# Whole tile loads, overlapping places for K, and products with a zero tile, in a one-token transformer block

## The chip, the cores and the metric

The kernel runs on one core of one Trainium2 chip. The metric is the device time in microseconds of one execution. Before the change it was 202.29 us, the median of three executions (202.23 to 202.43). "Span" below is the length of a profiled execution without its launch, 1.2 to 1.4 us shorter than the time in all executions but five (1.5 to 2.4 us there). The "granted clock" is the share of its full speed at which TensorE was let run; 0.50 is called half clock below.

## The reference

One new token goes through attention over a cache of 4096 keys and values in 32 heads, then through a gated feed-forward block. Cut to what matters:

```python
def reference(A_x, A_k_cache, A_v_cache, A_wq, A_wo, B_x, B_w_gate, B_w_up, B_w_down):
    # x: [1,1,640]; k_cache, v_cache: [1,32,4096,128]; wq: [640,4096]; wo: [4096,640]
    q = (layernorm(x) @ wq)                   # 32 heads of 128
    p = softmax(q . k_cache * 128**-0.5)      # 4096 scores a head
    h = x + (p . v_cache) @ wo
    g, u = layernorm(h) @ w_gate, layernorm(h) @ w_up     # 1728 wide
    return h + (gelu(g) * u) @ w_down
```

All of it is bf16. Nearly every byte is used once: 84.2 MB come from HBM, and 67 MB of them are K and V.

## The kernel before

Eight heads make a tile, and there are four tiles (NG). In a tile, partition 16h+p holds 256 keys of head h, so a tile of K or V is 64 KB in each partition, 8.39 MB in all. VectorE multiplies a quarter of K at a time with the query (`mult`, into `prod`). TensorE adds up the products in groups with an identity as weights (`fold`), VectorE finishes the sums (`total`), ScalarE takes the exponential, VectorE spreads it into `p_bd` (`block`), and TensorE multiplies that with V (`pv`). K has one buffer, filled in halves, and V has one buffer; all large loads are issued from SP (SyncE), in order.

```python
def load_k(j, s):          # K of tile j, half s
    landed["K", j, s] = P.dma("sync", k_all[:, HALF*s : HALF*s+HALF], src[:, HALF*s : HALF*s+HALF],
                              mults.get((j - 1, s, 1)))          # waits for that half's last multiplication
...
lp = P.loop("tensor", range(NG), [
    ("f00", lambda e, j: fold(e, 0), lambda j: [mults[j, 0, 0], reds[j - 1, 1] if j else qa], True),
    ("f01", lambda e, j: fold(e, 1), lambda j: [mults[j, 0, 1]], True),
    ("f10", lambda e, j: fold(e, 0), lambda j: [mults[j, 1, 0], reds[j, 0]], True),
    ("f11", lambda e, j: fold(e, 1), lambda j: [mults[j, 1, 1]], True),
    ("p0", lambda e, j: pv(e, 0), lambda j: [blocks[j, 0], landed["V", j, 0]], True),
    ("p1", lambda e, j: pv(e, 1), lambda j: [blocks[j, 1], seen[j]], True),
    ("h", lambda e, j: head_sum(e, j * 8), lambda j: [evs[j]], True)])
...
for j in range(NG):
    mult(j, 0, 0); mult(j, 0, 1)
    if j < NG - 1: load_k(j + 1, 0)
    mult(j, 1, 0); total(j, 0); mult(j, 1, 1)
    if j < NG - 1: load_k(j + 1, 1)
    block(j, 0); total(j, 1); block(j, 1)
    ...                                       # V of tile j+1, after pvs[j, 1]; the last V in halves
```

After the last tile come W_o (into K's buffer), the gate and up weights (into V's buffer, so after the last `pv`) and w_down, and their products with one column each.

The softmax here doesn't subtract the row's maximum and nothing guards it: scores larger than these inputs give would overflow.

Of the kernel before, what the change touches and what calls it, by code (L numbers as in the profile page):

```python
# [5 lines left out]
FP32 = mybir.dt.float32  # L6
BF16 = mybir.dt.bfloat16
ALU = mybir.AluOpType
ACTF = mybir.ActivationFunctionType
AX = mybir.AxisListType  # L10
# [3 lines left out]
DH = 128  # L14
# [6 lines left out]
NG = 4  # L21
# [143 lines left out]
def held(e, out, lhsT, rhs, start, stop):  # L165

    built = e.matmul(out, lhsT, rhs, start=start, stop=stop)  # L167
    old = built.ins
    bb = e.bass.cur_bb.bb
    new = mybir.InstMatmult(  # L170
        start_tensor_calc=old.start_tensor_calc, stop_tensor_calc=old.stop_tensor_calc, tile_size=old.tile_size,
        tile_position=old.tile_position, ldweights=False, name=old.name, engine=old.engine, debug=old.debug,
        ins=old.ins, outs=old.outs, sync_info=old.sync_info)
    insts = bb.instructions
    assert insts[-1].name == old.name
    del insts[-1]
    insts.append(new)
    return bass.BassInstruction(new)


def bass_sequential_preLN__gqa_block_cached__glu_gated_geglu__decode_kernel(nc, A_x, A_k_cache, A_v_cache, A_wq, A_wo, B_x, B_w_gate, B_w_up, B_w_down, out):
    sb = lambda name, shape, dt: nc.alloc_sbuf_tensor(name, shape, dt)
    k_all = sb("k_all", [128, 2 * 128 * DH], BF16)
    v_all = sb("v_all", [128, 256 * DH], BF16)
    prod = sb("prod", [128, 2, 64, DH], BF16)
    qb = sb("qb", [128, NG, DH], BF16)
    sc = sb("sc", [128, 128], FP32)
    pt = sb("pt", [128, 128], BF16)
    spare = sb("spare", [1, 1], FP32)
    own = sb("own", [128, 4], BF16)  # L190
    own8 = sb("own8", [128, 8], BF16)
    p_bd = sb("p_bd", [128, 2, 128, 8], BF16)
# [43 lines left out]
    ps_z = bank[7]  # L236
# [16 lines left out]
    landed = {}  # L253
    HALF = 128 * DH

    def load_k(j, s):
        src = A_k_cache[0, 8 * j:8 * j + 8, :, :].rearrange("h (p r) d -> (h p) (r d)", p=16)
        landed["K", j, s] = P.dma("sync", k_all[:, HALF * s:HALF * s + HALF], src[:, HALF * s:HALF * s + HALF],
                                  mults.get((j - 1, s, 1)))

    def load_v(j, lo, hi, *after, chan=None):
        src = A_v_cache[0, 8 * j:8 * j + 8, :, :].rearrange("h (p r) d -> (h p) (r d)", p=16)
        ev = P.dma("sync", v_all[:, HALF * lo:HALF * hi], src[:, HALF * lo:HALF * hi], *after, chan=chan)
        for i in range(lo, hi):
            landed["V", j, i] = ev

    load_k(0, 0)
    load_k(0, 1)


    c_xz = GP(lambda e: e.memset(xlnB[:, :, :], 0.0))
# [39 lines left out]
    def idle(eng, n):  # L311

        def fn(e):
            for _ in range(n):
                i = e.nop(hint="n", nofuse=True)
            return i
        return P.op(eng, fn)

    idle("tensor", 56)

    def x_cols(e):
        for c in range(5):
# [36 lines left out]
    AS = lambda fn, *d: P.op("scalar", fn, *d, chan="s")  # L359
    GS = lambda fn, *d: P.op("gpsimd", fn, *d, chan="s")  # L360
    qa = VR(lambda e: e.tensor_copy(qb[:, :, :].rearrange("p g d -> p (g d)"), ps_q), qd)  # L361
    load_v(0, 0, 2, qd, chan="V")


    reds, exps, blocks, evs, folds, seen = {}, {}, {}, {}, {}, {}

    def half(e, i, s, first=True):
        for n in range(8):
            mm = held if n or not first else lambda e, *a, **k: e.matmul(*a, **k)  # L369
            r = mm(e, bank[2 * i + s], id_b[:, :], prod[:, i, 32 * s:32 * s + 32, 16 * n:16 * n + 16], start=(n == 0), stop=(n == 7))  # L370
        return r

    def fold(e, i):
        half(e, i, 0)
        return half(e, i, 1, False)

    def pv(e, s):
        vt = tile3(v_all[:, HALF * s:HALF * s + HALF])
        for b in range(32):
            a = 32 * (b % 4)  # L380
            i = e.matmul(ps_o[a:a + 32, :], p_bd[:, s, 4 * b:4 * b + 4, :].rearrange("p g j -> p (g j)"),  # L381
                         vt[:, 4 * b:4 * b + 4, :], start=(s == 0 and b < 4), stop=(s == 1 and b >= 28))
        return i

    def head_sum(e, at):
# [2 lines left out]
                         start=(r == 0), stop=(r == 3))  # L388
        return i

    def mult(j, s, i):
        kt = tile3(k_all[:, HALF * s:HALF * s + HALF])
        mults[j, s, i] = VM(lambda e: e.tensor_tensor(  # L393
            out=prod[:, i, :, :], in0=kt[:, 64 * i:64 * i + 64, :],
            in1=qb[:, j, :].unsqueeze(1).to_broadcast([128, 64, DH]), op=ALU.mult),
            landed["K", j, s], qa, folds.get((j, 0, i) if s else (j - 1, 1, i)))

    def total(j, s):
        reds[j, s] = VR(lambda e: e.reduce_sum(sc[:, :], ps_f.rearrange("p (g d) -> p g d", d=16), axis=AX.X), folds[j, s, 1],  # L399
                        exps.get((j, 0) if s else (j - 1, 1)))  # L400
        exps[j, s] = AS(lambda e: e.activation(pt[:, :], sc[:, :], ACTF.Exp, bias=zero_t[:, 0:1],  # L401
                                               scale=INV_SQRT_DH, accum_out=RS[:, 2 * j + s:2 * j + s + 1]), reds[j, s], c_eps,
                        blocks.get((j, 0) if s else (j - 1, 1)))

    def block(j, s):
        blocks[j, s] = VB(lambda e: e.tensor_tensor(  # L406
            out=p_bd[:, s, :, :], in0=pt[:, :].unsqueeze(2).to_broadcast([128, 128, 8]),
            in1=own8[:, :].unsqueeze(1).to_broadcast([128, 128, 8]), op=ALU.mult), exps[j, s], c_own8, pvs.get((j - 1, s)))

    T(None, c_idb, c_hs)  # L410
    lp = P.loop("tensor", range(NG), [
        ("f00", lambda e, j: fold(e, 0), lambda j: [mults[j, 0, 0], reds[j - 1, 1] if j else qa], True),
        ("f01", lambda e, j: fold(e, 1), lambda j: [mults[j, 0, 1]], True),
        ("f10", lambda e, j: fold(e, 0), lambda j: [mults[j, 1, 0], reds[j, 0]], True),
        ("f11", lambda e, j: fold(e, 1), lambda j: [mults[j, 1, 1]], True),
        ("p0", lambda e, j: pv(e, 0), lambda j: [blocks[j, 0], landed["V", j, 0]], True),
        ("p1", lambda e, j: pv(e, 1), lambda j: [blocks[j, 1], seen[j]], True),
        ("h", lambda e, j: head_sum(e, j * 8), lambda j: [evs[j]], True)])
    for j in range(NG):
        for s in range(2):  # L420
# [3 lines left out]
    for j in range(NG):  # L424
        mult(j, 0, 0)
        mult(j, 0, 1)
        if j < NG - 1:
            load_k(j + 1, 0)
        mult(j, 1, 0)
        total(j, 0)  # L430
        mult(j, 1, 1)
        if j < NG - 1:
            load_k(j + 1, 1)
        block(j, 0)
        total(j, 1)
        block(j, 1)
        seen[j] = GS(lambda e: e.memset(spare[:, :], 0.0), landed["V", j, 1])  # L437
        if j < NG - 2:
            load_v(j + 1, 0, 2, pvs[j, 1], chan="V")
        elif j == NG - 2:  # L440
            load_v(j + 1, 0, 1, pvs[j, 1], chan="V")
            load_v(j + 1, 1, 2)
        evs[j] = AS(lambda e: e.copy(po_sb[:, :], ps_o), pvs[j, 1])  # L443

    rt = GP(lambda e: e.tensor_tensor(out=RT[:, :, :], in0=RS[:, :].unsqueeze(2).to_broadcast([128, 2 * NG, 8]),
# [1 line left out]
    def z_sum(e):  # L447
        for s in range(2):
# [9 lines left out]
    ap = V(lambda e: e.tensor_copy(aP[:, :], ps_z[:, 32:64]), sp)  # L458


    d_wo = [P.dma("sync", wo_sb[:, i:i + 16, :], A_wo[:, :].rearrange("(p i) n -> p i n", i=32)[:, i:i + 16, :], mults[NG - 1, 1, 1])
            for i in (0, 16)]
    wg_sb = v_all[:, 0:5 * DF].rearrange("p (c n) -> p c n", c=5)
    wu_sb = v_all[:, 5 * DF:10 * DF].rearrange("p (c n) -> p c n", c=5)
# [64 lines left out]
    g6 = V(lambda e: e.tensor_mul(gu[:, :], g_t[:, :], t1[:, :]), g8)  # L529
    g9 = V(lambda e: e.tensor_mul(hm[:, :], gu[:, :], ps_u[:, 0:15]), g6, up)  # L530

    idle("vector", 3)

    def down(ms, qs=range(4)):
        def fn(e):
            for m in ms:
# [52 lines left out]
```

## Time and profile before

| | before |
|---|---|
| time | 202.26 us |
| span of the profiled execution | 200.9 us |
| packets of the load queue, share of 16 engines' span | 97.8% |
| busy: TensorE, VectorE | 57%, 52% |
| mean granted TensorE clock | 0.795 |
| last V half seen, w_up seen, last of w_down seen | 171.34, 193.82, 198.50 us |

The prediction below shows the slices, the chain and the rows that matter. Two more lines of the view of the DMA queue's own waits show why VectorE and TensorE appear in a chain that is otherwise DMA; the columns are who waited, for what, us in total, times and the longest wait.

```profile
SPq L59 <- DVE prod L393: 99.6, 7, 24.3
SPq L59 <- PE psum L381: 43.9, 4, 15.0
```

SP waits for a buffer most of the time, 143.5 us in these two lines. In the kernel before, earlier loads were still in the queue while it waited: the packets of the queue fill 97.8% of the span.

### The profile page before, as it was taken

What the parts mean: (1) busy time and instruction counts of PE and PEld (TensorE: products, weight loads), DVE (VectorE), ACT (ScalarE), POOL (GpSimd) and SP (SyncE); (2) the same over time, 40 slices, a digit from 0 to 9 for tenths busy, and PEclk for the clock granted to TensorE, in tenths of its full rate; (3) what the DMA queues carried; (4) which work ended last, traced back from release to release, by engine and by line L of the source; (5) the groups of instructions that cost most, each with busy time, mean ns of one, the idle gap of its engine ahead of it and who ended that gap; (6) DMA issues with size and microseconds to landing.
All of it is one profiled execution on the core that took longest, in us unless ns stands there. A gap on an engine that the chain in (4) does not pass through costs nothing.

```text
span 200.9 us, 2025 instructions
## 1 busy us (share of the span) xinstructions
PE 115.3 (57%) x982; PEld 30.4 (15%) x738; DVE 103.6 (52%) x56; ACT 9.4 (5%) x27; POOL 6.7 (3%) x36
## 2 busy tenths in 40 slices
PE   0108019667094296696605938566088496674675
PEld 0103000000032000001300000023000001474574
DVE  0200197994601969945149799420798965120320
ACT  2100000000001000000100000001000000100100
POOL 6500000000000000000000000000000000000000
PEclk9999856999858559579965899969669879955555
DMA  8999999999899999999999999899999999999992
GB/s 326 449 406 437 431 450 424 417 431 499 385 444 417 424 522 417 417 417 411 417 424 424 489 457 444 378 411 424 424 450 437 431 444 391 432 436 414 423 402 107
DMA packets 3275, 84.31 MB, mean 420 GB/s; under 512 B 387, under 2 KB 582, under 8 KB 966
## 3 DMA queue, kind: packets, MB, share of 16 engines
q1 hardware_dynamic: 3266, 84.23, 97.8%
q8 instruction: 4, 0.07, 0.1%
q14 instruction: 1, 0.01, 0.0%
q10 hardware_dynamic: 4, 0.00, 0.0%
HBM read 84.23 MB, written 0.00 MB: 419 GB/s over the span
## 4 chain that ended last, share of the span: by engine, by line
DMA 66%; DVE 22%; PE 11%; issue 0%; ACT 0%; SPq 0%; DVEq 0%
DMA k_all<-in_A_k_cache_dram 56%; DVE prod L393 18%; DMA v_all<-in_B_w_up_dram 10%; PE psum L167 7%; DVE sc L399 3%; PE psum L516 1%; PE psum L539 1%; PE psum L381 1%; DVE p_bd L406 1%; PE psum L369 1%; SPq L59 0%; ACT pt L401 0%; ACT out_row L555 0%; DVE hm L530 0%; DVEq L114 0%
## 5 line engine op out<-in xcount | busy, mean ns | idle before, releaser
L393 DVE TENSOR_TENSOR prod<-k_all,qb 128x8192 bf16<-128x8192 bf16 x16 | 70.4, 4421 | 38.0 <-DMA k_all<-in_A_k_cache_dram 33.1
L167 PE MATMUL psum<-prod,id_b 128*128 128x512 bf16 x240 | 66.0, 437 | 0.0
L369 PE MATMUL psum<-prod,id_b 128*128 128x512 bf16 x16 | 7.3, 454 | 45.3 <-DVE prod L393 31.5
L381 PE MATMUL psum<-v_all,p_bd 128*32 128x512 bf16 x256 | 19.4, 464 | 14.2 <-DMA v_all<-in_A_v_cache_dram 11.0
L399 DVE TENSOR_REDUCE sc<-psum 128x128 f32<-128x2048 f32 x8 | 18.3, 2288 | 13.3 <-PE psum L167 13.3
L369 PEld LDWEIGHTS psum<-prod,id_b 128*128 128x128 bf16 x16 | 1.6, 99 | 99.8 <-DVE prod L393 59.4
L381 PEld LDWEIGHTS psum<-v_all,p_bd 128*32 128x32 bf16 x256 | 7.5, 114 | 38.5 <-DMA v_all<-in_A_v_cache_dram 21.8
L406 DVE TENSOR_TENSOR p_bd<-pt,own 128x1024 bf16<-128x1024 bf16 x8 | 9.8, 1222 | 2.2 <-ACT pt L401 2.2
L401 ACT ACTIVATE pt<-sc,zero_t 128x128 bf16<-128x128 f32 x8 | 3.2, 402 | 135.9 <-DVE sc L399 135.9
L352 PE MATMUL psum<-v_all,xlnB 128*32 128x512 bf16 x40 | 4.5, 631 | 6.7 <-DMA v_all<-in_A_wq_dram 6.7
L486 PE MATMUL psum<-aP,k_all 128*128 128x1 bf16 x160 | 6.7, 178 | 2.7 <-DMA k_all<-in_A_wo_dram 2.7
L486 PEld LDWEIGHTS psum<-aP,k_all 128*128 128x128 bf16 x160 | 6.6, 131 | 2.8 <-DMA k_all<-in_A_wo_dram 2.8
L516 PE MATMUL psum<-hlnT,v_all 128*128 128x1 bf16 x150 | 5.5, 173 | 1.2 <-DMA v_all<-in_B_w_up_dram 1.2
L387 PE MATMUL psum<-hs,po_sb 128*128 128x8 f32 x32 | 4.2, 258 | 3.2 <-ACT po_sb L443 3.2
L437 POOL MEMSET spare<- 1x1 f32 x4 | 0.4, 88 | 162.8 <-DMA v_all<-in_A_v_cache_dram 162.8
L361 DVE CAST qb<-psum 128x512 bf16<-128x512 f32 x1 | 0.7, 692 | 9.7 <-PE psum L352 9.7
L516 PEld LDWEIGHTS psum<-hlnT,v_all 128*128 128x128 bf16 x150 | 5.3, 120 | 1.8 <-DMA v_all<-in_B_w_up_dram 1.3
L492 DVE COPY hT<-psum 128x5 f32<-128x5 f32 x1 | 0.2, 166 | 9.6 <-PE psum L486 9.6
L387 PEld LDWEIGHTS psum<-hs,po_sb 128*128 128x128 f32 x32 | 3.9, 191 | 5.1 <-issue 5.1
L323 PE MATMUL psum<-one_bf,x_row 1*128 1x1 bf16 x5 | 0.4, 177 | 7.1 <-DMA x_row<-in_A_x_dram 7.1
L326 DVE COPY xx<-psum 128x5 f32<-128x5 f32 x1 | 0.2, 165 | 7.5 <-PE psum L323 7.5
L443 ACT COPY po_sb<-psum 128x512 f32<-128x512 f32 x4 | 2.3, 585 | 22.3 <-PE psum L381 22.3
(71 smaller groups left out, 28.6 us busy)
## 6 DMA issues: line engine op xcount, KB each, us to landing
k_all<-in_A_k_cache_dram SPq DMA_DIRECT2D x8, 4096.0 KB, 29.1
v_all<-in_A_v_cache_dram SPq DMA_DIRECT2D x2, 4096.0 KB, 28.5
v_all<-in_A_wq_dram SPq DMA_DIRECT2D x1, 5120.0 KB, 15.2
k_all<-in_A_wo_dram SPq DMA_DIRECT2D x2, 2560.0 KB, 17.4
v_all<-in_B_w_gate_dram SPq DMA_DIRECT2D x1, 2160.0 KB, 15.0
v_all<-in_B_w_up_dram SPq DMA_DIRECT2D x1, 2160.0 KB, 19.8
k_all<-in_B_w_down_dram SPq DMA_DIRECT2D x1, 800.0 KB, 22.3
k_all<-in_B_w_down_dram SPq DMA_DIRECT2D x1, 640.0 KB, 20.9
```

Of the source, the lines that this page charges most:

```text
L167: built = e.matmul(out, lhsT, rhs, start=start, stop=stop)
L352: i = e.matmul(ps_q[32 * t:32 * t + 32, :], xlnB[:, c, 32 * a:32 * a + 32], wq_j[:, c, t, a, :, :], start=(c == 0 and a == 0), stop=(c == ...
L369: mm = held if n or not first else lambda e, *a, **k: e.matmul(*a, **k)
L381: i = e.matmul(ps_o[a:a + 32, :], p_bd[:, s, 4 * b:4 * b + 4, :].rearrange("p g j -> p (g j)"), vt[:, 4 * b:4 * b + 4, :], start=(s == 0 a ...
L387: i = e.matmul(ps_a[:, bass.ds(at, 8)], po_sb[:, 128 * r:128 * r + 128], hs[:, r, :], start=(r == 0), stop=(r == 3))
L393: mults[j, s, i] = VM(lambda e: e.tensor_tensor(out=prod[:, i, :, :], in0=kt[:, 64 * i:64 * i + 64, :], in1=qb[:, j, :].unsqueeze(1).to_br ...
L399: reds[j, s] = VR(lambda e: e.reduce_sum(sc[:, :], ps_f.rearrange("p (g d) -> p g d", d=16), axis=AX.X), folds[j, s, 1], exps.get((j, 0) i ...
L401: exps[j, s] = AS(lambda e: e.activation(pt[:, :], sc[:, :], ACTF.Exp, bias=zero_t[:, 0:1], scale=INV_SQRT_DH, accum_out=RS[:, 2 * j + s:2 ...
L406: blocks[j, s] = VB(lambda e: e.tensor_tensor(out=p_bd[:, s, :, :], in0=pt[:, :].unsqueeze(2).to_broadcast([128, 128, 8]), in1=own8[:, :]. ...
L443: evs[j] = AS(lambda e: e.copy(po_sb[:, :], ps_o), pvs[j, 1])
L486: r = e.matmul(ps_p[:, c:c + 1], wo_sb[:, i, c::5], aP[:, i:i + 1], start=False, stop=(i == 31), skip_group_check=True)
L516: i = e.matmul(ps[:, m:m + 1], ws, hlnT[:, c:c + 1], start=(c == 0 and m == 0), stop=(c == 4), skip_group_check=True)
```

## The change

The intent: fewer and larger loads, a K buffer of 80 KB in which the next K may be fetched when three quarters of the present one are used, and products with a tile of zeros in TensorE's waits, which were to keep its clock up. The core of the diff:

```diff
-    k_all = sb("k_all", [128, 2 * 128 * DH], BF16)
+    k_all = sb("k_all", [128, 320 * DH], BF16)
+    K_AT = [0, 64 * DH, 0, 64 * DH]
-    def load_k(j, s):
+    def load_k(j):
+        parts = ((0, 1), (1, 2)) if j == NG - 1 else ((0, 2),)
+        for lo, hi in parts:
+            ev = P.dma("sync", k_all[:, K_AT[j] + HALF * lo:K_AT[j] + HALF * hi], src[:, HALF * lo:HALF * hi],
+                       mults.get((j - 1, 1, 0)), chan=None if lo else "K")
 ...
-    idle("tensor", 56)
+    idle("tensor", 22)
 ...
+    def warm(e, n, load=False):
+        for k in range(n):
+            mm = e.matmul if load and k == 0 else lambda *a, **kw: held(e, *a, **kw)
+            r = mm(ps_z, none_b[:, :], none_b[:, :].unsqueeze(1).to_broadcast([128, 4, 128]), start=True, stop=True)
 ...
     lp = P.loop("tensor", range(NG), [
+        ("wa", lambda e, j: warm(e, 8, True), lambda j: [landed["K", j, 0]], False),
         ("f00", ...), ("f01", ...),
+        ("wb", lambda e, j: warm(e, 12), lambda j: [], False),
         ("f10", ...), ("f11", ...),
-        ("p0", lambda e, j: pv(e, 0), lambda j: [blocks[j, 0], landed["V", j, 0]], True),
-        ("p1", lambda e, j: pv(e, 1), lambda j: [blocks[j, 1], seen[j]], True),
+        ("wc", lambda e, j: warm(e, 14), lambda j: [], False),
+        ("p0", lambda e, j: pv(e, 0), lambda j: [blocks[j, 1], landed["V", j]], True),
+        ("p1", lambda e, j: pv(e, 1), lambda j: [], True),
 ...
         mult(j, 0, 0)
         mult(j, 0, 1)
+        mult(j, 1, 0)
         if j < NG - 1:
-            load_k(j + 1, 0)
-        mult(j, 1, 0)
+            load_k(j + 1)
         total(j, 0)
         mult(j, 1, 1)
 ...
-    d_wo = [... mults[NG - 1, 1, 1]) for i in (0, 16)]
+    d_wo = [... mults[NG - 1, 0, 1]) for i in (0, 16)]
 ...
-    idle("vector", 3)
```

(The small GpSimd instruction `seen`, which stood for the landing of V's second half, is gone with that half; the quarters of even tiles are taken in another order, so that the one outside the next tile's place comes last; the second total of an even tile is two instructions. All V loads are whole.)

More of the change, by code (lines that the diff above doesn't have):

```diff
@@ L188, in bass_sequential_preLN__gqa_block_cached__glu_gated_geglu__decode_kernel @@
     pt = sb("pt", [128, 128], BF16)
-    spare = sb("spare", [1, 1], FP32)
     own = sb("own", [128, 4], BF16)
@@ L254, in bass_sequential_preLN__gqa_block_cached__glu_gated_geglu__decode_kernel, with load_v @@
     HALF = 128 * DH
-    def load_k(j, s):
+    K_AT = [0, 64 * DH, 0, 64 * DH]
+    def load_k(j):
         src = A_k_cache[0, 8 * j:8 * j + 8, :, :].rearrange("h (p r) d -> (h p) (r d)", p=16)
-        landed["K", j, s] = P.dma("sync", k_all[:, HALF * s:HALF * s + HALF], src[:, HALF * s:HALF * s + HALF],
-                                  mults.get((j - 1, s, 1)))
-    def load_v(j, lo, hi, *after, chan=None):
-        src = A_v_cache[0, 8 * j:8 * j + 8, :, :].rearrange("h (p r) d -> (h p) (r d)", p=16)
-        ev = P.dma("sync", v_all[:, HALF * lo:HALF * hi], src[:, HALF * lo:HALF * hi], *after, chan=chan)
-        for i in range(lo, hi):
-            landed["V", j, i] = ev
-    load_k(0, 0)
-    load_k(0, 1)
+        parts = ((0, 1), (1, 2)) if j == NG - 1 else ((0, 2),)
+        for lo, hi in parts:
+            ev = P.dma("sync", k_all[:, K_AT[j] + HALF * lo:K_AT[j] + HALF * hi], src[:, HALF * lo:HALF * hi],
+                       mults.get((j - 1, 1, 0)), chan=None if lo else "K")
+            for i in range(lo, hi):
+                landed["K", j, i] = ev
+    def load_v(j, *after):
+        src = A_v_cache[0, 8 * j:8 * j + 8, :, :].rearrange("h (p r) d -> (h p) (r d)", p=16)
+        landed["V", j] = P.dma("sync", v_all[:, 0:2 * HALF], src, *after, chan="V")
+    load_k(0)
     c_xz = GP(lambda e: e.memset(xlnB[:, :, :], 0.0))
@@ L361, in bass_sequential_preLN__gqa_block_cached__glu_gated_geglu__decode_kernel @@
     qa = VR(lambda e: e.tensor_copy(qb[:, :, :].rearrange("p g d -> p (g d)"), ps_q), qd)
-    load_v(0, 0, 2, qd, chan="V")
-    reds, exps, blocks, evs, folds, seen = {}, {}, {}, {}, {}, {}
+    load_v(0, qd)
+    reds, exps, blocks, evs, folds = {}, {}, {}, {}, {}
     def half(e, i, s, first=True):
@@ L370, in half @@
             r = mm(e, bank[2 * i + s], id_b[:, :], prod[:, i, 32 * s:32 * s + 32, 16 * n:16 * n + 16], start=(n == 0), stop=(n == 7))
+        return r
+    def warm(e, n, load=False):
+        for k in range(n):
+            mm = e.matmul if load and k == 0 else lambda *a, **kw: held(e, *a, **kw)
+            r = mm(ps_z, none_b[:, :], none_b[:, :].unsqueeze(1).to_broadcast([128, 4, 128]), start=True, stop=True)
         return r
@@ L389, in head_sum, with half_of @@
         return i
+    def half_of(j, s):
+        return s if j % 2 else 1 - s
     def mult(j, s, i):
-        kt = tile3(k_all[:, HALF * s:HALF * s + HALF])
+        c = (2 * s + i) if j % 2 else (2 + i, 1 - i)[s]
+        kt = tile3(k_all[:, K_AT[j]:K_AT[j] + 2 * HALF])
         mults[j, s, i] = VM(lambda e: e.tensor_tensor(
-            out=prod[:, i, :, :], in0=kt[:, 64 * i:64 * i + 64, :],
+            out=prod[:, i, :, :], in0=kt[:, 64 * c:64 * c + 64, :],
             in1=qb[:, j, :].unsqueeze(1).to_broadcast([128, 64, DH]), op=ALU.mult),
-            landed["K", j, s], qa, folds.get((j, 0, i) if s else (j - 1, 1, i)))
+            landed["K", j, half_of(j, s)], qa, folds.get((j, 0, i) if s else (j - 1, 1, i)))
     def total(j, s):
-        reds[j, s] = VR(lambda e: e.reduce_sum(sc[:, :], ps_f.rearrange("p (g d) -> p g d", d=16), axis=AX.X), folds[j, s, 1],
-                        exps.get((j, 0) if s else (j - 1, 1)))
+        free = exps.get((j, 0) if s else (j - 1, 1))
+        g16 = lambda lo, hi: ps_f[:, lo:hi].rearrange("p (g d) -> p g d", d=16)
+        if s and j % 2 == 0:
+            V(lambda e: e.reduce_sum(sc[:, 64:128], g16(0, 1024), axis=AX.X), folds[j, s, 1], free)
+            reds[j, s] = VR(lambda e: e.reduce_sum(sc[:, 0:64], g16(1024, 2048), axis=AX.X))
+        else:
+            reds[j, s] = VR(lambda e: e.reduce_sum(sc[:, :], g16(0, 2048), axis=AX.X), folds[j, s, 1], free)
         exps[j, s] = AS(lambda e: e.activation(pt[:, :], sc[:, :], ACTF.Exp, bias=zero_t[:, 0:1],
@@ L405, in block @@
     def block(j, s):
+        hf = half_of(j, s)
         blocks[j, s] = VB(lambda e: e.tensor_tensor(
-            out=p_bd[:, s, :, :], in0=pt[:, :].unsqueeze(2).to_broadcast([128, 128, 8]),
-            in1=own8[:, :].unsqueeze(1).to_broadcast([128, 128, 8]), op=ALU.mult), exps[j, s], c_own8, pvs.get((j - 1, s)))
-    T(None, c_idb, c_hs)
+            out=p_bd[:, hf, :, :], in0=pt[:, :].unsqueeze(2).to_broadcast([128, 128, 8]),
+            in1=own8[:, :].unsqueeze(1).to_broadcast([128, 128, 8]), op=ALU.mult), exps[j, s], c_own8, pvs.get((j - 1, 1)))
+    T(None, c_idb, c_hs, c_none)
     lp = P.loop("tensor", range(NG), [
+        ("wa", lambda e, j: warm(e, 8, True), lambda j: [landed["K", j, 0]], False),
         ("f00", lambda e, j: fold(e, 0), lambda j: [mults[j, 0, 0], reds[j - 1, 1] if j else qa], True),
         ("f01", lambda e, j: fold(e, 1), lambda j: [mults[j, 0, 1]], True),
+        ("wb", lambda e, j: warm(e, 12), lambda j: [], False),
         ("f10", lambda e, j: fold(e, 0), lambda j: [mults[j, 1, 0], reds[j, 0]], True),
         ("f11", lambda e, j: fold(e, 1), lambda j: [mults[j, 1, 1]], True),
-        ("p0", lambda e, j: pv(e, 0), lambda j: [blocks[j, 0], landed["V", j, 0]], True),
-        ("p1", lambda e, j: pv(e, 1), lambda j: [blocks[j, 1], seen[j]], True),
+        ("wc", lambda e, j: warm(e, 14), lambda j: [], False),
+        ("p0", lambda e, j: pv(e, 0), lambda j: [blocks[j, 1], landed["V", j]], True),
+        ("p1", lambda e, j: pv(e, 1), lambda j: [], True),
         ("h", lambda e, j: head_sum(e, j * 8), lambda j: [evs[j]], True)])
@@ L426, in bass_sequential_preLN__gqa_block_cached__glu_gated_geglu__decode_kernel @@
         mult(j, 0, 1)
+        mult(j, 1, 0)
         if j < NG - 1:
-            load_k(j + 1, 0)
-        mult(j, 1, 0)
+            load_k(j + 1)
         total(j, 0)
         mult(j, 1, 1)
-        if j < NG - 1:
-            load_k(j + 1, 1)
         block(j, 0)
@@ L436, in bass_sequential_preLN__gqa_block_cached__glu_gated_geglu__decode_kernel @@
         block(j, 1)
-        seen[j] = GS(lambda e: e.memset(spare[:, :], 0.0), landed["V", j, 1])
-        if j < NG - 2:
-            load_v(j + 1, 0, 2, pvs[j, 1], chan="V")
-        elif j == NG - 2:
-            load_v(j + 1, 0, 1, pvs[j, 1], chan="V")
-            load_v(j + 1, 1, 2)
+        if j < NG - 1:
+            load_v(j + 1, pvs[j, 1])
         evs[j] = AS(lambda e: e.copy(po_sb[:, :], ps_o), pvs[j, 1])
@@ L458, in bass_sequential_preLN__gqa_block_cached__glu_gated_geglu__decode_kernel @@
     ap = V(lambda e: e.tensor_copy(aP[:, :], ps_z[:, 32:64]), sp)
-    d_wo = [P.dma("sync", wo_sb[:, i:i + 16, :], A_wo[:, :].rearrange("(p i) n -> p i n", i=32)[:, i:i + 16, :], mults[NG - 1, 1, 1])
+    d_wo = [P.dma("sync", wo_sb[:, i:i + 16, :], A_wo[:, :].rearrange("(p i) n -> p i n", i=32)[:, i:i + 16, :], mults[NG - 1, 0, 1])
             for i in (0, 16)]
```

## The prediction

> **What bounds the kernel now.** I read the page first (busy shares and the forty slices), then the chain that ended last in order of time, then the waits of the DMA queue, then the timeline. The slices and the queue table carry the main point:
>
> ```profile
> PEclk9999856999858559579965899969669879955555
> DMA  8999999999899999999999999899999999999992
> GB/s 326 449 406 437 431 450 424 417 431 499 385 444 417 424 522 417 417 417 411 417 424 424 489 457 444 378 411 424 424 450 437 431 444 391 432 436 414 423 402 107
> q1 hardware_dynamic: 3266, 84.23, 97.8%
> ```
>
> The DMA row is at 9 from end to end; only the first and the last slice fall. The queue's packets took 97.8% of sixteen engines' span: 0.978 x 200.9 = 196.5 us of transfer, leaving 4.4 us for the start, before data flows, and for the end, after the last weight lands. The chain agrees:
>
> ```profile
> 0.46 24.41 DMA k_all<-in_A_k_cache_dram
> ...
> 33.68 30.91 DMA k_all<-in_A_k_cache_dram
> ...
> 73.40 29.97 DMA k_all<-in_A_k_cache_dram
> ...
> 124.58 27.28 DMA k_all<-in_A_k_cache_dram
> ...
> 173.99 19.78 DMA v_all<-in_B_w_up_dram
> ```
>
> Columns are start, length, what. A chain piece such as "33.68 30.91" runs from issue to landing; most of it is queueing behind V. So the 22% of VectorE in the chain does not mean that a faster VectorE would pay: its release of a buffer only sets when a transfer joins a queue that still has work. The landings show it. The two products with p_bd of tiles 0 to 3 first see V at 54.92, 93.70 and 132.48, and the last V half is seen at 171.34:
>
> ```profile
> 54.92 0.09 POOL L437 MEMSET spare<- 1x1 f32 x1 [46.68 <-DMA v_all<-in_A_v_cache_dram]
> 93.70 0.09 POOL L437 MEMSET spare<- 1x1 f32 x1 [38.69 <-DMA v_all<-in_A_v_cache_dram]
> 132.48 0.09 POOL L437 MEMSET spare<- 1x1 f32 x1 [38.69 <-DMA v_all<-in_A_v_cache_dram]
> 171.34 0.09 POOL L437 MEMSET spare<- 1x1 f32 x1 [38.77 <-DMA v_all<-in_A_v_cache_dram]
> ```
>
> That is 38.78, 38.78 and 38.86 us for a tile of K and V (16.78 MB): 432.6 GB/s, three times the same although the clock and the waits on chip differ from tile to tile. **The bound is the stream of bytes**, and the end is what hangs on the last weights.
>
> [...] The trace's packet records [...]: median 2.419 us for a packet of 65,536 bytes (the whole V tiles), 1.214 us for one of 32,768 bytes (K halves): 2 x 1.214 - 2.419 = 0.009 us lost per split row. [...] the granted clock is 0.50 or 1.00 in most 2 us windows, and sixteen products with id_b take 3.6 us at 46.1 but 6.2 us at 69.1. [...]
>
> **The change part by part.**
>
> *Whole loads.* K of tiles 0 to 2 and V of tile 3 lose their split: four tiles, 8 rows per DMA engine each, 0.009 us per row: 4 x 8 x 0.009 = 0.29 us. Thirteen loads become nine; each ends in a 4-byte packet of 0.009 us per engine: 0.04 us. Sum 0.33 us off the stream. Check: a pair is now 16 x 1.214 + 8 x 2.419 = 38.78 us, exactly the measured period, and will be 16 x 2.419 = 38.70 us. This is the only part on the path that sets the end.
>
> *K must land whole before VectorE starts.* Work on a tile begins about 9.7 us later than in before (half of 19.4 us). With T for K's landing, and the durations of these rows:
>
> ```profile
> L393 DVE TENSOR_TENSOR prod<-k_all,qb 128x8192 bf16<-128x8192 bf16 x16 | 70.4, 4421 | 38.0 <-DMA k_all<-in_A_k_cache_dram 33.1 <-PE psum L167 4.9
> L399 DVE TENSOR_REDUCE sc<-psum 128x128 f32<-128x2048 f32 x8 | 18.3, 2288 | 13.3 <-PE psum L167 13.3
> L406 DVE TENSOR_TENSOR p_bd<-pt,own 128x1024 bf16<-128x1024 bf16 x8 | 9.8, 1222 | 2.2 <-ACT pt L401 2.2
> ```
>
> three multiplications end at T+13.2 at full clock; total T+15.5; fourth multiplication T+19.9; block T+21.1; its fold ends T+23.5; total T+25.8; exponential 0.6, block 1.2: T+27.6; 64 products with V at 1.95 us per 32: T+31.5. That work is busy beside the transfers and must only fit in the 38.7 us period. It does.
>
> *Alternating places.* The next K shares three of its tile's four quarters, so it is issued at T+13.2, while V (19.4 us) runs until T+19.4: 6.2 us to spare. The next V is issued at T+31.5, the K before it ends at T+38.7: 7.2 us. The first V waits for the query, as now (19.82), well before K ends near 34.5. For K of tile 3 the halves return, the first landing at about T-9.7, so that the W_o load is issued (T-9.7, plus two multiplications of 8.8) some 20 us before V is through. No hole should open in the stream.
>
> *Zero products.* 34 per tile: 136 x 0.22 us = 30 us of TensorE time at full clock (0.43 us each at half). They stand in waits: 8 while VectorE makes the first products (at half clock 3.4 us against 4.42), 12 (2.6 us) between the folds, where TensorE waits about 3 us for the total, 14 (3.0 us) before V's products, which wait 4.1 us for total, exponential and block. Their gain is folds at 3.6 rather than 5.6 to 6.2 us and V's products at 3.9 rather than 6.5 us. Off the path of the end: 0 us.
>
> *The end.* All V products of tile 3 now wait for one load. In before half were done early:
>
> ```profile
> 171.66 1.91 PE L381 MATMUL psum<-v_all,p_bd 128*32 128x512 bf16 x32 [2.42 <-DVE p_bd L406]
> ...
> 183.53 3.36 PE L486 MATMUL psum<-aP,k_all 128*128 128x1 bf16 x80 [2.67 <-DMA k_all<-in_A_wo_dram]
> ...
> 193.82 2.75 PE L516 MATMUL psum<-hlnT,v_all 128*128 128x1 bf16 x75 [1.21 <-DMA v_all<-in_B_w_up_dram]
> ```
>
> The first of these lines is the second run of 32, begun 0.3 us after V was seen. In the changed kernel V lands near 171.0, its products end near 174.9 to 177.5 instead of 173.6; the 3.5 us of small steps after them put the first W_o products at 178.5 to 181, instead of 177.5. The second half of W_o lands near 183.2 anyway; even at the late end it shifts the gate products by 1.2 us, and the up products still begin with the landing of w_up, now near 193.45. So 0 us, and 7.1 us after that landing remain. The two split totals cost VectorE some tenths in tiles 0 and 2, hidden; the three NOPs taken from VectorE are nothing.
>
> *Sum*: 202.29 - 0.33 = 201.96, rounded to 201.95 us.
>
> **The rivals.** *(A) A hole in the stream.* If zeros did not keep the clock up, folds of 6.2 us would put the third multiplication's end at T+15.1, the last fold's at T+29.8, V's products' at about T+40.4: 1.7 us beyond the end of the next K, plus the start of a transfer, for three tiles: 5 to 9 us, some 208 us. For it speaks that in before many folds ran at half clock; against it [...] one slow fold alone fits in the 6 to 7 us to spare. *(B) The end becomes longer*: V's products late and cold, with W_o's and the gate's behind them. The slack of 1.2 us at w_up is all but used up at half clock; a slip would be 0.5 to 1.5 us, to 203 us. *(C) More gain than the packets*: an earlier W_o issue or a warm clock shortens the end. Against it: W_o waits in the queue anyway, and the clock is 0.50 from 178 us on, in products with one column, where no filler stands. At best 1 us, to 201 us.
>
> **Range and chances.** The main path gives 201.95, with the runs of before within 0.2 us. (C) sets the low end at 201.4, a mild (B) the high end at 202.8. A gain of over 2% needs 4 us, and only 4.4 us of the span are not transfer at all: 1%. A loss of over 2% needs (A): 4%. Within 2%: 95%.
>
> **What would show it.** Right: DMA share still near 98%; landings of V 38.7 us apart, no slice of DMA under 8 between first and last; packets of K at 65,536 bytes; W_up seen near 193.5; TensorE busy up by 15 to 25 us, and a mean granted clock above the 0.795 of before, with the time nearly unchanged. Wrong: a V or K issue in the DMA queue's waits later than the end of the load before it, a dip in the DMA row in the middle, or up products waiting on VectorE rather than on w_up.

The sum came to 202.29 - 0.33 = 201.96 us: the 0.33 us are worked out from packet records of the kernel before, 0.009 us for each of 32 split rows and for each of four 4-byte packets. `idle("tensor", ...)` are NOPs before the loop: 34 fewer, as the loop grows by 35 instructions, so that its end stays where it was.

## The result, and the profile after

The changed kernel takes **202.17 us**, median of six executions (202.03 to 202.71), against 202.26 us (202.18 to 202.43). The ratio is 0.9998, with a 95% interval of 0.9985 to 1.0011: no difference that can be told. A ratio here is the mean time of one kernel's executions over that of the other's in the same rounds, so it is not quite the ratio of the medians quoted.

The slices of the page after, and the row of the load queue (clock, busy share of the DMA engines; packets, MB, share):

```profile
PEclk9999999999999855899999599999999999965555
DMA  9999999999999999999999999899999999999992
q1 hardware_dynamic: 2690, 84.23, 97.7%
```

The DMA row is as full as before, in 2690 packets instead of 3266. The clock is up through most of the attention part (mean of the span 0.892 against 0.795), and at half in the same last stretch. TensorE works more, for nothing that the end needs; its groups in the changed kernel (count | busy us, mean ns | idle before):

```profile
L167 PE MATMUL psum<-prod,id_b 128*128 128x512 bf16 x240 | 55.9, 387 | 0.0
L167 PE MATMUL psum<-none_b 128*128 128x512 bf16 x132 | 34.9, 419 | 0.0
```

The folds took 66.0 us in the same group before. So 10.1 us of folds are saved and 37 us of zeros paid (34.9, and 2.2 for the first one of each tile); TensorE's busy time goes from 115.3 to 135.1 us.

The chain that ended last still runs from load to load (start, length, what):

```profile
0.45 34.01 DMA k_all<-in_A_k_cache_dram
...
47.61 26.59 DMA k_all<-in_A_k_cache_dram
...
88.52 24.38 DMA k_all<-in_A_k_cache_dram
...
144.15 26.89 DMA v_all<-in_A_v_cache_dram
...
175.23 18.28 DMA v_all<-in_B_w_up_dram
```

The timeline shows how much room the issues have (start, length, engine, instruction, idle before it):

```profile
65.71 0.33 SPq L59 DMA_DIRECT2D v_all<-in_A_v_cache_dram  x1
...
74.22 8.76 DVE L405 TENSOR_TENSOR prod<-k_all,qb 128x8192 bf16<-128x8192 bf16 x2 [12.24 <-DMA k_all<-in_A_k_cache_dram]
...
106.56 0.33 SPq L59 DMA_DIRECT2D v_all<-in_A_v_cache_dram  x1
...
112.92 8.76 DVE L405 TENSOR_TENSOR prod<-k_all,qb 128x8192 bf16<-128x8192 bf16 x2 [10.10 <-DMA k_all<-in_A_k_cache_dram]
```

V of tile 1 is issued 8.5 us before the K ahead of it is seen, V of tile 2 6.4 us before. VectorE now waits 12 and 10 us for the whole K of tiles 1 and 2. And the end, in the timeline of the changed kernel:

```profile
171.18 3.64 PE L389 MATMUL psum<-v_all,p_bd 128*32 128x512 bf16 x64 [1.81 <-DMA v_all<-in_A_v_cache_dram]
...
178.61 3.36 PE L501 MATMUL psum<-aP,k_all 128*128 128x1 bf16 x80
183.28 3.36 PE L501 MATMUL psum<-aP,k_all 128*128 128x1 bf16 x80 [1.31 <-DMA k_all<-in_A_wo_dram]
...
193.55 2.76 PE L531 MATMUL psum<-hlnT,v_all 128*128 128x1 bf16 x75 [1.22 <-DMA v_all<-in_B_w_up_dram]
...
198.42 0.23 PEld L552 LDWEIGHTS psum<-k_all,hm 128*1 128x1 bf16 x12 [0.38 <-DMA k_all<-in_B_w_down_dram]
```

The last of these lines in the kernel before:

```profile
198.50 0.23 PEld L539 LDWEIGHTS psum<-k_all,hm 128*1 128x1 bf16 x12 [0.21 <-DMA k_all<-in_B_w_down_dram]
```

All V products run after the last landing, the first W_o products start 1.1 us later than before, the second ones wait for their load as they did, and w_up is seen 0.27 us earlier (193.55 for 193.82). But the last wait for w_down ends at 198.42 instead of 198.50: of the 0.27 us only 0.08 are left. Profiles of the runs below repeat this: w_up was seen at 193.76 and 193.79 in before_zero and before_v_whole and at 193.52 and 193.46 in after_again and nops_86, the last of w_down at 198.45 and 198.46, and at 198.42 and 198.33.

In the packet records the load queue's packets sum to 196.25 us an engine, 0.29 less than before (196.54), for 0.33 forecast. before_zero has the same 3266 packets as before and 196.40, so two profiles with equal packets can differ by 0.14.

### The profile page after: what moved, and what is told of

It is laid out like the page before. It is cut to its first block, busy times and chain, and to the rows that moved or that the text cites. A ratio compares the mean times of both kernels' runs of the same rounds, so it can differ in the third digit from the quotient of the medians.

```text
span 200.9 us, 2115 instructions
## 1 busy us (share of the span) xinstructions
PE 135.1 (67%) x1118; PEld 29.8 (15%) x742; DVE 103.6 (52%) x58; ACT 9.4 (5%) x27; POOL 7.4 (4%) x32
## 3 DMA queue, kind: packets, MB, share of 16 engines
q1 hardware_dynamic: 2690, 84.23, 97.7%
## 4 chain that ended last, share of the span: by engine, by line
DMA 65%; DVE 23%; PE 11%; issue 0%; ACT 0%; SPq 0%; DVEq 0%
DMA k_all<-in_A_k_cache_dram 42%; DVE prod L405 20%; DMA v_all<-in_A_v_cache_dram 13%; DMA v_all<-in_B_w_up_dram 9%; PE psum L167 4%; PE psum L389 4%; PE psum L531 1%; PE psum L552 1%; DVE sc L417 1%; DVE p_bd L424 1%; DVE sc L414 1%; DVE sc L415 1%; PE psum L371 0%; SPq L59 0%; ACT pt L418 0%
## 5 line engine op out<-in xcount | busy, mean ns | idle before, releaser
L167 PE MATMUL psum<-prod,id_b 128*128 128x512 bf16 x240 | 55.9, 387 | 0.0
L167 PE MATMUL psum<-none_b 128*128 128x512 bf16 x132 | 34.9, 419 | 0.0
L378 PE MATMUL psum<-none_b 128*128 128x512 bf16 x4 | 2.2, 549 | 26.1 <-DMA k_all<-in_A_k_cache_dram 26.1
L389 PE MATMUL psum<-v_all,p_bd 128*32 128x512 bf16 x256 | 14.5, 380 | 5.4 <-DVE p_bd L424 3.6
L417 DVE TENSOR_REDUCE sc<-psum 128x128 f32<-128x2048 f32 x6 | 13.7, 2286 | 5.2 <-PE psum L167 5.2
L371 PE MATMUL psum<-prod,id_b 128*128 128x512 bf16 x16 | 6.4, 400 | 9.5 <-DVE prod L405 6.7
L389 PEld LDWEIGHTS psum<-v_all,p_bd 128*32 128x32 bf16 x256 | 6.7, 97 | 37.5 <-DVE p_bd L424 31.6
L460 POOL TENSOR_TENSOR RT<-RS,own 128x64 f32<-128x64 f32 x1 | 1.3, 1324 | 161.0 <-ACT pt L418 161.0
L414 DVE TENSOR_REDUCE sc<-psum 128x64 f32<-128x1024 f32 x2 | 2.4, 1224 | 5.2 <-PE psum L167 5.2
```

The costliest lines, as they stand in the source:

```text
L167: built = e.matmul(out, lhsT, rhs, start=start, stop=stop)
L371: mm = held if n or not first else lambda e, *a, **k: e.matmul(*a, **k)
L389: i = e.matmul(ps_o[a:a + 32, :], p_bd[:, s, 4 * b:4 * b + 4, :].rearrange("p g j -> p (g j)"), vt[:, 4 * b:4 * b + 4, :], start=(s == 0 a ...
L414: V(lambda e: e.reduce_sum(sc[:, 64:128], g16(0, 1024), axis=AX.X), folds[j, s, 1], free)
L417: reds[j, s] = VR(lambda e: e.reduce_sum(sc[:, :], g16(0, 2048), axis=AX.X), folds[j, s, 1], free)
```

## The experiments

Two theories about why nothing moved. **Stream**: the time is the stream of bytes plus what hangs on the last weights; the parts of the change trade slack against slack. **Rivals**: a part of the change gains and another loses (zeros gain and late V products lose, or the reverse), so that the sum is near zero by chance; or the kernel is held by something on the chip. Each part was undone or done alone, and costs were magnified. Where "holes" are given in us, they are counted from the packet records: the time in which fewer than 16 DMA engines had a packet, weighted by the share without one.

| run | median us | ratio to before (95%) |
|---|---|---|
| after_again | 202.15 | 1.0009 (0.9987 to 1.0031) |
| no_zero_products | 205.09 | 1.0138 (1.0099 to 1.0177) |
| no_alternation | 212.77 | 1.0497 (1.0456 to 1.0537) |
| v_in_16 | 206.59 | 1.0213 (1.0198 to 1.0228) |
| before_zero | 202.20 | 0.9999 (0.9985 to 1.0013) |
| before_v_whole | 202.24 | 0.9996 (0.9983 to 1.0010) |
| zeros_42 | 209.00 | 1.0317 (1.0278 to 1.0356) |
| zeros_70 | 227.35 | 1.1246 (1.1229 to 1.1263) |
| zeros_ahead | 202.44 | 1.0015 (1.0001 to 1.0029) |
| wd_lo_16 | 203.23 | 1.0060 (1.0046 to 1.0074) |
| nops_86 | 202.21 | 1.0004 (0.9990 to 1.0018) |
| k_halves | 203.42 | 1.0052 (1.0031 to 1.0073) |

The medians of before in the four calls were 202.22, 202.30, 202.22 and 202.22 us. All kernels gave correct results.

### after_again: the changed kernel once more

No edit.

> The changed kernel itself, five rounds. Theory (the stream of bytes is the bound, and the change only takes 0.29 to 0.33 us of packets off it): 202.0, ratio 0.9984. Rival (the saving is lost before the end, because the last piece of w_down lands at nearly the old time, 198.42 against 198.50): 202.2, ratio 0.9996 or nearer to 1.

202.15 us, executions from 201.95 to 203.50. With the six of the first measurement, nine of twelve lie between 201.95 and 202.25 (mean 202.12), three at 202.70, 202.71 and 203.50. So in most executions the gain is about 0.1 us, less than the spread of before itself (202.16 to 202.64), and in some there is a loss. W_up was seen at 193.52 and the last of w_down at 198.42, as in the first profile: the rival of this run holds, most of the saving is gone by the last weights.

### no_zero_products: undo the zeros

```diff
-    idle("tensor", 22)
+    idle("tensor", 57)
-        ("wa", ... warm(e, 8, True) ...), ("wb", ... warm(e, 12) ...), ("wc", ... warm(e, 14) ...),
```

> The changed kernel without the 34 products with the zero tile, 35 NOPs added before the loop so that the rest of the program stays where it was. Theory (there are 6 to 7 us to spare for each issue, and TensorE's clock falls only in part): folds of 5.6 to 6.2 us first in each tile, granted clock near 0.80, V issued at some T+33 to T+37 after K's landing at T, no hole, 202.1 to 202.4. Rival A of the prediction (without a full clock the whole loads do not fit in their period): holes of 1 to 3 us in the DMA row before V of tiles 1 to 3, 205 to 211 us. [...]

205.09 us, from 203.68 to 206.37; the granted clock fell to 0.772 in the profiled one. Both theories were half right. In tile 1 two folds and V's products ran at half clock (fifteen products of a fold in 5.75 and 6.10 us, where folds at full clock take 3.40; 0.50 from 108 to 110 us, amid V's products), V was issued 0.8 us before K was seen to have landed, and the load queue ran dry. The timeline, and the table of stretches (length, busy us of each engine, then clock, DMA share, GB/s; a packet counts where it starts, so the row says that none started in these 2 us):

```profile
91.91 6.10 PE L167 MATMUL psum<-prod,id_b 128*128 128x512 bf16 x15
...
111.99 0.33 SPq L59 DMA_DIRECT2D v_all<-in_A_v_cache_dram  x1
...
112.76 8.76 DVE L405 TENSOR_TENSOR prod<-k_all,qb 128x8192 bf16<-128x8192 bf16 x2 [7.18 <-DMA k_all<-in_A_k_cache_dram]
```

```profile
110.00:112.00 2.00, 1.95 (x28) 0.67 (x20) 0.00 (x0) 0.00 (x0) 0.00 (x0) 0.75 0.00 0
```

The hole is 2.1 us, one tile only. But this execution was 3.3 us longer, and its end tells the rest:

```profile
174.08 6.18 PE L389 MATMUL psum<-v_all,p_bd 128*32 128x512 bf16 x64 [4.25 <-DVE p_bd L424]
...
194.49 5.32 PE L528 MATMUL psum<-hlnT,v_all 128*128 128x1 bf16 x150
```

One fold of tile 3 was at half clock too (6.00 us for fifteen products at 160.38). V's products wait for p_bd, not for V, and take 6.18 us instead of 3.64. From there on everything is late, and the gate and up products run as one group of 150 without waiting for w_up. The chain that ended last contains no load after 160 us. So rival B of the prediction is real as soon as the zeros are taken away: the changed kernel needs them. Only one execution was profiled, the one with the lowest clock but one. The mean clock does not order the six: one at 0.855, as high as in many executions of the changed kernel, took 204.51 us. What holds up those executions is not shown.

### no_alternation: undo the places

```diff
-    K_AT = [0, 64 * DH, 0, 64 * DH]
+    K_AT = [0, 0, 0, 0]
-                       mults.get((j - 1, 1, 0)), chan=None if lo else "K")
+                       mults.get((j - 1, 1, 1)), chan=None if lo else "K")
-    d_wo = [... mults[NG - 1, 0, 1]) ...]
+    d_wo = [... mults[NG - 1, 1, 0]) ...]
```

(and `load_k(j + 1)` after the fourth multiplication.)

> The changed kernel with every K tile at the same place, so that the next K is issued after the fourth multiplication (about T+19.6) and not after the third. Theory (V's last packet ends about T+18.9, a transfer issued into an empty queue starts about 1.0 us after its issue): a hole of 1.6 us before K of tiles 1, 2 and 3, a little more where the folds are cold, 5 to 6 us in all: 207 to 208 us. Rival (an issue some tenths late is hidden by the depth of the queue, or by faster transfer afterwards): 202 to 203.5 us.

212.77 us, 10.5 more than before; the theory's direction, and twice its size. The issue that comes after V is through, and the stretch in which almost no packet starts (same columns as above):

```profile
54.36 0.33 SPq L59 DMA_DIRECT2D k_all<-in_A_k_cache_dram  x1
```

```profile
52.00:54.00 2.00, 1.76 (x9) 0.00 (x0) 2.00 (x1) 0.00 (x0) 0.00 (x0) 1.00 0.04 8
```

The engines start to run out at 52.45 us, and all sixteen have a packet again at 56.26, 1.9 us after the issue. The first packet starts at 55.32, 0.96 us after the issue, as I had put; that the other engines follow only later, I had left out (1.7 and 1.3 us in the other two holes). The three holes are 2.81, 2.16 and 3.90 us, the last one longer (I put that down to a fold at half clock before its issue; no view quoted here shows it): 8.87 us. Besides, the packets sum to 197.95 us an engine instead of 196.25: they are slower, by 1.70 us. The sixteen packets that start first after a hole account for about that: they take 3.04 and 3.03 us in the mean where 2.42 is usual, and 1.87 where 1.21 is usual in the third hole. Together 10.57, and this execution's span is 211.5 - 200.9 = 10.6 us longer. With whole loads, the alternating places are not a refinement, they are what makes the load order possible.

### v_in_16: many more packets

```diff
-        landed["V", j] = P.dma("sync", v_all[:, 0:2 * HALF], src, *after, chan="V")
+        n = 2 * HALF // 16
+        for i in range(16):
+            landed["V", j] = P.dma("sync", v_all[:, n*i:n*i+n], src[:, n*i:n*i+n], *after, chan="V")
```

> The changed kernel with each V tile loaded in 16 pieces of 4 KB a row, on one semaphore that is awaited in full. Theory (9 ns for each packet and each closing 4-byte packet, on each DMA engine): 4 tiles x (128 - 8) = 480 packets and 60 closings more per engine, 540 x 0.009 = 4.9 us: 207.0 us. Rival (the cost of a packet is hidden by the next one in the engine, and the 0.33 us of the prediction are no gain at all): 202 to 203 us.

206.59 us, 4.4 more than the changed kernel's 202.15. The DMA row stays full (no hole), so this is the packets: 4.44 / 540 = 8.2 ns each, for 9 forecast. Packets do cost time at the end, nearly what was forecast. Their records sum to more, 202.84 us an engine, 6.58 above the changed kernel; about 2.0 us of that are packets whose records overlap. For the 36 packets that the change saves on each engine (32 rows and 4 closings) that gives 36 x 8.2 = 0.30 us.

### before_zero: the zeros alone

```diff
-    idle("tensor", 56)
+    idle("tensor", 21)
+        ("wa", lambda e, j: warm(e, 8, True), lambda j: [], False),
         ("f00", ...), ("f01", ...),
+        ("wb", lambda e, j: warm(e, 12), lambda j: [], False),
         ("f10", ...), ("f11", ...),
+        ("wc", lambda e, j: warm(e, 14), lambda j: [], False),
```

> The kernel before with the 34 zero products in its loop (8 ahead of the first fold, without a wait; 12 between the folds; 14 before V's products), 35 NOPs fewer before it. Theory (zeros only keep the clock up, and in the kernel before no transfer waits for a fold): granted clock up from 0.80 to 0.85 or more, time 202.1 to 202.3, ratio 1.000. Rival (a fuller clock is itself worth something, at the end or in the waits of VectorE): 201.0 to 201.8.

202.20 us, ratio 0.9999, at a clock of 0.865. Before the change, a fuller clock was worth nothing: the loads in halves kept the queue filled at either clock (its packets sum to 196.40 us an engine here, 196.54 in before).

### before_v_whole: the last V in one load, alone

```diff
-        if j < NG - 2:
+        if j < NG - 1:
             load_v(j + 1, 0, 2, pvs[j, 1], chan="V")
-        elif j == NG - 2:
-            load_v(j + 1, 0, 1, pvs[j, 1], chan="V")
-            load_v(j + 1, 1, 2)
```

> The kernel before with V of tile 3 in one load instead of two. Theory (8 packets and one closing fewer per engine, some 0.07 us; all 64 products with V after the landing, hidden behind W_o): 202.15, ratio 0.9997, no difference that can be told from zero. Rival B of the prediction (V's products late lengthen the end): 202.7 to 203.7.

202.24 us, ratio 0.9996. In its profile V's products take 5.32 us from 171.30 on, where 64 of them take 3.64 in the changed kernel (until 174.93 the weights of four come every 0.43 us, as in before from 54.92 on, at a granted clock of 0.50), gate and up weights are issued at 176.67 instead of 173.61, and w_up is still seen at 193.79. Waiting for the whole V costs nothing, as forecast.

### zeros_42 and zeros_70: how much room V's issue has

```diff
-        ("wc", lambda e, j: warm(e, 14), lambda j: [], False),
+        ("wc", lambda e, j: warm(e, 42), lambda j: [], False),     # or 70
```

> The changed kernel with 42 instead of 14 zero products before V's products, a delay of some 5 us put on purpose before V's issue in each tile. Theory (the next V joins the queue 8.5 us before K has landed in the changed kernel; a hole opens only where less than some 3 us are left, as the run without zero products showed with 0.8 us left and a hole of 2.1): V issued some 3.5 us before K lands, no hole, or one of some tenths in a tile whose first fold is cold: 202.1 to 203.0. Rival (TensorE's busy time bounds the kernel): 3 x 5 = 15 us more, 217.

> The changed kernel with 70 instead of 14 zero products before V's products, some 11 us of delay. Theory (the slack is used up): V issued some 2.3 us after K has landed, holes of some 5 us before V of tiles 1 to 3, and 2 to 3 us more at the end where W_o's products begin late: 217 to 222 us. Rival (slack larger than reckoned): 202 to 210.

209.00 and 227.35 us. For 42 I had forecast 202.1 to 203.0, and that was wrong; for 70, 217 to 222, too low as well. The timeline of the run with 42:

```profile
72.06 0.33 SPq L59 DMA_DIRECT2D v_all<-in_A_v_cache_dram  x1
...
74.04 13.10 DVE L405 TENSOR_TENSOR prod<-k_all,qb 128x8192 bf16<-128x8192 bf16 x3 [10.47 <-DMA k_all<-in_A_k_cache_dram]
...
181.00 3.64 PE L389 MATMUL psum<-v_all,p_bd 128*32 128x512 bf16 x64
...
184.68 0.34 SPq L59 DMA_DIRECT2D v_all<-in_B_w_gate_dram  x1
...
198.86 5.36 PE L531 MATMUL psum<-hlnT,v_all 128*128 128x1 bf16 x150
```

V was issued 6.3 us later than in the changed kernel, 2.0 us before K was seen at 74.04: 1.2 us of the delay are a first fold at half clock (4.99 us for fifteen products, 3.40 in the next fold), which I had allowed only some tenths, and that opened a hole of 1.1 us. The larger part is at the end, which I had not worked out for this run at all: tile 3's zeros push V's products from 171.2 to 181.0, the gate weights are issued when the queue is empty (hole 1.4 us), and the up products no longer wait for w_up. In tile 2 of this run V was issued 4.2 us before K was seen (110.03 and 114.27), and no hole opened. So the room in front of V's issue in tile 1 is some 5 us (a hole of 1.1 at a delay of 6.3), while the room at the end is smaller. With 70 the holes before V of tiles 1 to 3 are 5.7, 1.1 and 3.4 us, and the one at the end is 8 us, where 2 to 3 had been allowed. The rival (TensorE's busy time as the bound) would give 15 us and is not needed.

### zeros_ahead: keep the clock up through the wait for K

```diff
-    idle("tensor", 22)
+    idle("tensor", 6)
-        ("wa", lambda e, j: warm(e, 8, True), lambda j: [landed["K", j, 0]], False),
+        ("w0", lambda e, j: warm(e, 16, True), lambda j: [], False),
+        ("wa", lambda e, j: warm(e, 8), lambda j: [landed["K", j, 0]], False),
```

> The changed kernel with 16 more zero products at the start of each tile, ahead of the wait for K. Theory (the few slow executions of the changed kernel, 202.7 and 203.5, are those in which a clock at half speed in the first fold makes V or K late; kept warm, they vanish): all executions within 201.9 to 202.3, median 202.1. Rival (those executions come from something else, as an outlier of 202.6 in the kernel before suggests): spread as in the changed kernel.

202.44 us, from 202.19 to 202.83. The granted clock rose to 0.90 to 0.91 (0.84 to 0.89 in the changed kernel). My theory of the slow executions did not hold: the spread is still there, and the median is 0.3 us higher. The profile shows the room at the end being used:

```profile
180.89 6.58 PE L502 MATMUL psum<-aP,k_all 128*128 128x1 bf16 x160
...
193.66 2.75 PE L532 MATMUL psum<-hlnT,v_all 128*128 128x1 bf16 x75 [0.48 <-DMA v_all<-in_B_w_up_dram]
```

The zeros delay tile 3, W_o's products start 2.3 us later than in the changed kernel and then run through without a wait, and the up products' wait for w_up shrinks from 1.22 to 0.48 us. Half a microsecond more, and the end would be the bound.

### wd_lo_16 and nops_86: where the saving is lost at the end

```diff
-    for o in (0, 1, 2, 3, 32, 33, 34, 35):        # eight loads over 4 partitions
-        ... wd_lo[o:o + 13:4, :, :] ...
+    for lo in (0, 32):                            # two loads over 16 partitions
+        d_wp = P.dma("sync", wd_lo[lo:lo + 16, :, :],
+                     B_w_down[lo:lo + 32, :].rearrange("(r s) n -> s r n", r=2), c_wd, chan="wp")
```

> The changed kernel with the low rows of w_down in two loads over 16 partitions instead of eight loads over 4, so that they may spread over all DMA engines. Theory (the saving was lost at the end because the last weights wait for a few DMA engines that carry more packets; 8 x (2 x 55 + 9) ns = 0.95 us on four of them, 0.24 us on each if spread): w_down lands 0.4 to 0.7 us earlier, 201.4 to 201.8. Rival (the engines that end last are late for another reason, the instruction fetch at 196.4): 202.1, no change.

```diff
-    idle("tensor", 22)
+    idle("tensor", 86)
```

> The changed kernel with 64 NOPs more before the loop, so that the last fetch of instructions falls earlier, near 195 us instead of 196.4. Theory of the fetch (16 KB that take 1.0 us on one DMA engine just before the last weights make that engine the last): the landing of w_down moves by some tenths, 201.8 to 202.4. Theory of the uneven engines (a fetch costs its engine the same wherever it falls): 202.1, within 0.1 of the changed kernel.

The first took 203.23 us, 1.1 more than the changed kernel: the theory falls, in the other direction. The number of packets is the same (2690, which fits sixteen 4-byte packets at the end of each load over 16 partitions, for four at the end of each over 4); w_up is seen at 194.61 instead of 193.55, and the gate and up packets sum to 10.90 us an engine instead of 10.38. Why the spread load slows what follows it, these runs do not settle.

The second took 202.21 us. The instruction fetch before the last weights (16 KB, 1.05 us in the changed kernel) did move from 196.35 to 195.42 us, and the last of w_down was seen at 198.33 instead of 198.42: nothing that can be told from the spread. So neither of my two ideas explains where 0.2 us go between w_up and the last of w_down. What the packet records show is that the sixteen DMA engines end at different times: in the changed kernel all are at work 2.2 us before the last packet of weights ends, 9 at 1.3 us, 4 at 0.7 us (in the kernel before 16, 10 and 6). The end waits for the slowest (the last packet of weights ends at 198.33, the last wait for w_down at 198.42), and a saving in the mean need not reach it; that this is where the 0.2 us went is not shown.

### k_halves: undo the whole K loads

```diff
-        parts = ((0, 1), (1, 2)) if j == NG - 1 else ((0, 2),)
+        parts = ((0, 1), (1, 2))
```

> The changed kernel with every K tile in two loads again, places and zero products kept. Theory (whole loads are worth 9 ns for each packet saved, three K tiles x 8 rows and three closings): 27 x 0.009 = 0.24 us more stream, W_up's landing 0.2 to 0.25 us later, 202.3 to 202.45. Rival (the saving never reaches the end): 202.15, as the changed kernel.

203.42 us, and not as forecast: two executions at 202.19 and 202.31, four from 203.28 to 203.70. The profiled one was the 202.19. There w_up is seen at 193.74, 0.19 later than in the changed kernel, and the packets sum to 196.62 us for 196.25, as the theory of packets has it:

```profile
193.74 2.67 PEld L531 LDWEIGHTS psum<-hlnT,v_all 128*128 128x128 bf16 x75 [1.28 <-DMA v_all<-in_B_w_up_dram]
```

No slow execution of this kernel was profiled. They have a slightly lower mean clock (0.842 to 0.846, against 0.859 and 0.861), which would fit a late tile 3 as in no_zero_products, but that is argued and not shown. The run is not a clean return to halves either: even tiles start with the second half, so in tiles 0 and 2 VectorE still waits for the whole K (until 113.08 in tile 2). So what the whole K loads save in the profiled execution is 0.2 us in w_up's landing; why this mixture takes 1.3 us more in four of six executions is open, and so are the three slow executions of the changed kernel.

Whole K loads alone and the alternating places alone were not tried in the kernel before. No run was faster than both kernels by more than its spread.

## Why the prediction was right

The time, 202.17 us, lies in the range of 201.4 to 202.8, 0.2 us above the predicted 201.95. That alone proves little, as the old 202.26 lies in the range too; the mechanism has to be looked at. Point by point (T is the landing of a tile's K):

- **The bound is the stream**: right. v_in_16 lengthens the stream by 540 packets an engine and the time by 4.4 us, without a hole; before_zero makes TensorE's clock fuller and the time stays.
- **Packets, 0.33 us**: right in the stream, where the records have 0.29 and w_up's landing moved by 0.27. Mis-sized at the end: the sum took the whole saving over to the time, and 0.08 us arrived in the profile, 0.1 in the medians. The step that carried it from w_up to the end ("7.1 us after that landing remain") failed: the remainder was 7.3 (200.86 - 193.55). The last of w_down comes with the slowest DMA engine; why that one gained less is not settled.
- **The timetable of a tile**: right. K is issued at T+13.1 in tile 0 (T+13.2 forecast) and T+14.3 in tile 1, where the first fold was at half clock (4.92 us for fifteen products); V at T+31.2 and T+32.3 (T+31.5). From K of tile 1 to K of tile 2 it is 38.70 us (74.22 to 112.92), as forecast.
- **Slack of 6 to 7 us**: right that no hole opens, generous in size. It was counted to the landing of the load ahead. In zeros_42 the first engines ran out at 71.73, 2.3 us before K was seen, and the first packet of V started 0.97 us after its issue; so some 3.3 us of the room cannot be used (an estimate from these numbers; no hole with 4.2 us left, one of 1.1 with 2.0).
- **The zeros, 0 us on the path of the end**: right only together with the rest. Alone they are worth nothing (0.9999), but without them the changed kernel takes 205.09. They took 37 us of TensorE, for 30 at full clock.
- **The end, 0 us**: right. V's products ended at 174.8 (174.9 forecast), W_o's began at 178.61 (178.5), and the 1.2 us of room at w_up are there: 1.22.
- **Rival A, 5 to 9 us without a kept clock**: right as a mechanism, wrong in size. The run without zeros lost 2.9 us, by one hole of 2.1 in its profile and not three, and by rival B at the same time. That zeros do keep the clock up is shown: 0.86 to 0.87 in all executions of before_zero, 0.77 to 0.82 in those of before.
- **Rival B, an end 0.5 to 1.5 us longer**: did not happen in the changed kernel's profiles, but zeros_ahead, zeros_42 and no_zero_products show it as the nearest limit.
- **Rival C, more gain than the packets**: did not happen. No execution of the changed kernel was under 201.95 us.

The large edit moved the time so little because each part pays for another. Whole loads save 0.3 us and give up VectorE's head start of half a K load; the alternating places give the stream back what this would cost (10.5 us without them), and the zeros give TensorE the pace that the shorter time needs (2.9 us without them).

## What to carry to other kernels

When one queue of loads is busy from end to end, count a change by what it does to that queue: packets saved, and issues that come in time (here no hole opened with 4.2 us left to the landing of the load ahead, and one of 1.1 us with 2.0 left). Here work that was late on another engine cost nothing while the queue still had loads (in before_v_whole the gate weights were issued 3.1 us later, at a ratio of 0.9996). Where its release came after the queue was empty, it cost the hole, the restart and slower packets: in no_alternation 8.87 us in three holes, each with 1.3 to 1.9 us from the issue until all sixteen engines had a packet, and 1.70 us more of packet time. And try a filler both ways, alone in the old kernel and taken out of the new one: here the zeros were worth nothing in the one and 2.9 us in the other.
